# A hand-ordered two-layer kernel: list figures and ranks, weight preparation by pairs of blocks, sums in place, and a residual that stays on chip

## The chip, the cores and the metric

The kernel runs on one core of a Trainium2 chip. The metric is the device time of one execution in microseconds. Three executions of the kernel before took 1379.39, 1375.03 and 1376.81 us, a median of 1376.81. One further execution was profiled; its own time was 1382.9 us.

A core has five engines that run side by side, each through its own instructions in order: TensorE (PE in the profile; its weight loads are PEld), VectorE (DVE), ScalarE (ACT), GpSimd (POOL) and SyncE (SP), which in this kernel issues nearly all transfers between the chip's memory (SBUF) and device memory. Matmul results go into the eight banks of PSUM.

## The reference

The same two blocks, with the same weights, are applied twice to an activation of 2048 tokens by 640 columns, all in float32:

```python
    x = A_x
    x = x + _A_ref(_layernorm(x, axis=-1), A_wqkv, A_wo)
    x = x + _B_ref(_layernorm(x, axis=-1), B_w1, B_b1, B_w2, B_b2)
    x = x + _A_ref(_layernorm(x, axis=-1), A_wqkv, A_wo)
    x = x + _B_ref(_layernorm(x, axis=-1), B_w1, B_b1, B_w2, B_b2)
```

`_A_ref` is linear attention with 32 heads of 20 columns: q, k, v = x @ wqkv; phi(t) is t + 1 where t > 0 and exp(t) elsewhere, plus 1e-6; for each head the output is phi(q) @ (phi(k)^T v), divided by phi(q) times the sum of phi(k) over the tokens; then @ wo. `_B_ref` is a feed-forward block of 1728 columns: h = relu(x @ w1 + b1) squared, then h @ w2 + b2.

## The kernel before, in words

**Precision.** A float32 matrix is split into a high part in a shorter format (ScalarE copies it) and the rest as a low part (VectorE subtracts), and a product is three matmuls: high by low, low by high, high by high. `split` (L284) does this; on the way a split is always one ScalarE instruction and then one VectorE instruction.

**Tiles.** The 2048 tokens are 16 tiles of 128 rows. Four tiles make a group, so there are four groups.

**Attention, first half: the token loop (L901 to L1090).** For each tile t: layer norm, transpose, k and q by matmuls (`part`, whose products are issued in `mm3`, L574), phi of both, and the sums over tokens: G = x^T k (`g_part`), GT (`gt_part`, every second tile), and acc, the sum of phi(k) (`k_post`, L857). phi(q) is stored to device memory. In some tiles (`LATE`) the q part is left for later (`late_q`). The order of the instructions on each engine is that of the program text. The loop's tile 15 also splits wo (`wo_high`, `wo_low`), whose pieces `load_vo` (L748) loads in tiles 13 to 15. After the loop acc is split (`ah`) and multiplied by ones, on the way to the denominators; G becomes the per-head products and then one 640 by 640 matrix M per layer.

**Weight preparation, layer 0 only.** Beside the token loop `Prep` (L412) loads w1 and w2 in pieces, combines and splits them and stores the split units to device memory, from where both layers later reload them. Two neighbouring column blocks of w1 make a pair with four units: wE and wF are split as loaded; then four GpSimd operations (`sums`, L443) combine the two blocks, and wH and wG are split from that. The remaining w1 and w2 pieces are one unit each: 36 units in all, in an order `todo`. `PREP` says how many units each tile takes. In tile t a unit's load for tile t + 1 is issued (`load`), ScalarE and VectorE split this tile's units (`high`, `low`), and at the start of the next tile `store` puts the issue of their stores on SP's queue, where each waits for VectorE's low part. After that store the tile's other transfers are issued: kept q/k weights (`keep_kq`), from tile 13 on phi(q) (`b_load_pq`, four pieces of a tile each) and the pieces of wv and wo (`load_vo`).

**Between the halves.** For the first group, attention's output is multiplied by M and added to the input (`b_x1`), normalized, transposed (tiles 0 and 1 by block moves, 2 and 3 by TensorE in `f_trans`, L1352) and split (`f_split`). The feed-forward block uses one level of Strassen's scheme, so sums of transposed tiles are formed for pairs of tiles (`t_sums`, L1336, four VectorE operations into two fresh buffers tu and tv of the ring "f") and split (`t_split`). The ring "f" has twelve buffers of one tile (`F_BUFS`); an instruction that needs a thirteenth waits until one is free.

**Feed-forward and the rest of attention: an order planned as a list (L1896 to L2287).** For each group, 14 column blocks of h: blocks 12 and 13 directly (`fc1`, L1461), the others in six Strassen blocks of two, each in five segments with copies and adds between them (`Strassen`, L1482). Each block of h is then multiplied by its part of w2 (`fc2_tile`, L1638) into five accumulators of the group. While a group is in work, the attention output of the next groups' tiles is made (`q_line`, `pair_line` with products in one PSUM bank, `x_line`). The order on every engine is worked out when the program is built, by `Clock` (L81): each strand of work is a `Line`, a generator that yields its next step with the engine and a length; `Clock.next` takes for each engine the step with the smallest (start rounded to 0.1 us, rank), and `Clock.run` does the same for TensorE by (wait, rank). The steps are then issued in that order. The lengths are figures in the code: `cost`, `pe_cost`, and for transfers `go` (L150):

```python
                start = max(start, self.lanes.pop(0))
                self.t["DMA"] = max(self.t["DMA"], start + 1.3) + each / 0.39
                line.got = self.got = self.t["DMA"] + 0.7 + HOP
                self.lanes.append(line.got)
                start += 0.08
```

`lanes` are eight: an issue waits for the transfer that was issued eight before it. On the chip SP's queue is in order: an issue that waits holds up everything behind it.

**Weights in the feed-forward block.** `uses` (L370) is the order in which units are reloaded; `Units` (L483) reloads the next one (L503) as soon as TensorE has done with a buffer. There are three buffers, then a fourth, and a fifth ("b") after the attention pools are closed.

**The residual.** For the second half, x after attention is needed once more, with b2 added. `x_line` stores it for the later groups (`x1_keep`, L847); for the first group `f_bias` (L839) adds b2 in place in the tile's "f" buffer, stores it to `x1d`, and `x1_load` (L1749) reloads the group's four tiles into `x1s[g]` (L1752). `x1_line` does the reload for every group, and fc2's last block (L2222) waits for it. b2 is also held as a column, `b2col` (L268), one value per partition, loaded by `late_consts` and used by `preset`.

## Time and profile before

| | |
|---|---|
| median of three runs | 1376.81 us |
| the profiled execution, its own time | 1382.9 us |
| its span in the trace | 1381.2 us |
| VectorE, ScalarE, GpSimd busy | 982.9, 770.5, 147.2 us |
| moved by DMA | 316.11 MB, 229 GB/s over the span |
| mean granted TensorE clock | 0.994 |

How to read the profile: a line of the timeline or of a group names the kernel's line, the engine, the operation, what it writes and reads (out<-in, without buffer numbers) and the shapes; "x6" means six instructions merged. In square brackets stands how long the engine was idle before, and what ended that (the releaser, found from the semaphores). A timeline line begins with its start and its length in us. SPq is SP's sequencer; a DMA line there is the issue of a transfer, not the transfer. The token loop of layer 0 lies up to about 200 us, its feed-forward block from about 260 to 700, the token loop of layer 1 from there to about 880, its feed-forward block from about 940 to the end.

### The profile page before, as it was taken

Reading aid. Unit: us, or ns where it says so; the run is one execution under the profiler, and the core shown is the slowest. Engines: PE = TensorE matmul, PEld = TensorE weight load, DVE = VectorE, ACT = ScalarE, POOL = GpSimd, SP = SyncE. Lnnn points to the kernel's source line nnn. Section 1 sums busy time; section 2 is a strip of 40 time slices with the busy share of each in tenths; the row PEclk is TensorE's granted clock in tenths of the full one; section 3 lists DMA queues with packets and bytes.
Section 4 is the critical chain, followed back from the end, with each engine's and each line's share of the span. In section 5 each row is a group of like instructions: output and inputs, shape, how many; then the busy total and the mean of one; then the engine's idle time right before and its main releaser. Section 6 shows DMA issues by size and latency. Waiting matters only on the chain.

```text
span 1381.2 us, 21322 instructions
## 1 busy us (share of the span) xinstructions
PE 1337.4 (97%) x7616; PEld 1180.7 (85%) x7616; DVE 982.9 (71%) x1928; ACT 770.5 (56%) x1753; POOL 147.2 (11%) x196
## 2 busy tenths in 40 slices
PE   9999989989999999999999999999899999999999
PEld 8888879878888879888888889997788888898887
DVE  8888968887887787354256678799788876874323
ACT  5888845646664655446336687565365644554421
POOL 2334310000000000000012232100000000000000
PEclk9999999999999999999999999999999999999999
DMA  6679685397779768698731114166877788587684
GB/s 200 226 267 333 245 274 181 123 350 240 250 248 307 282 201 307 239 375 306 266 127 44 58 39 132 52 193 229 304 242 221 253 303 265 184 298 273 229 313 175
DMA packets 120240, 316.11 MB, mean 229 GB/s; under 512 B 15110, under 2 KB 40326, under 8 KB 119462
## 3 DMA queue, kind: packets, MB, share of 16 engines
q1 hardware_dynamic: 118622, 312.06, 65.4%
q10 hardware_dynamic: 1512, 2.69, 0.7%
q8 instruction: 60, 0.98, 0.3%
q14 instruction: 46, 0.38, 0.1%
HBM read 251.28 MB, written 64.85 MB: 229 GB/s over the span
## 4 chain that ended last, share of the span: by engine, by line
PE 71%; DMA 12%; DVE 11%; issue 2%; SPq 2%; ACT 1%; POOL 1%; ACTq 0%; DVEq 0%; POOLq 0%
PE PS L574 25%; PE PS L1659 21%; PE PS L1510 15%; PE PS L1520 4%; DMA pqt<-pq 4%; DMA u<-kept_wH 2%; PE PS L1476 2%; DMA u<-kept_w 2%; DMA u<-kept_wG 1%; SPq L773 1%; DMA u<-kept_wE 1%; PE PS L1188 1%; DVE bn L524 1%; DVE uprep L407 1%; PE PS L927 1%
## 5 line engine op out<-in xcount | busy, mean ns | idle before, releaser
L1659 PE MATMUL PS<-u,h 128*128 128x512 f32 x1318 | 346.1, 397 | 1.4 <-ACT s L1532 0.7
L562 ACT ACTIVATE z<-y 32x160 f32<-32x160 f32 x767 | 256.1, 334 | 88.4 <-DVE y L549 69.3
L574 PE MATMUL PS<-kq,xT 128*128 128x320 f32 (+2 forms) x1575 | 283.4, 334 | 4.3 <-DVE r L686 3.5
L1659 PEld LDWEIGHTS PS<-u,h 128*128 128x128 f32 x1318 | 241.1, 190 | 50.3 <-DMA u<-kept_w 1.0
L574 PEld LDWEIGHTS PS<-kq,xT 128*128 128x128 f32 x1575 | 250.0, 188 | 31.5 <-DVE r L686 3.8
L1510 PE MATMUL PS<-tx,u 128*128 128x256 f32 x1152 | 162.7, 284 | 11.1 <-DMA u<-kept_wH 5.9
L1510 PEld LDWEIGHTS PS<-tx,u 128*128 128x128 f32 x1152 | 151.4, 192 | 16.9 <-DMA u<-kept_wH 6.5
L1588 ACT ACTIVATE hr<-PS,b1sb 128x512 f32<-128x512 f32 x104 | 71.2, 685 | 140.9 <-PE PS L1520 123.2
L1510 PEld LDWEIGHTS PS<-xTb,u 128*128 128x128 f32 x864 | 120.5, 189 | 20.1 <-DVE PS L1552 6.8
L1510 PE MATMUL PS<-xTb,u 128*128 128x256 f32 x864 | 127.4, 283 | 7.2 <-DVE PS L1552 4.6
L574 PE MATMUL PS<-kh,xh 128*128 128x512 f32 x480 | 126.9, 398 | 0.0
L529 POOL TENSOR_SCALAR rs<-mv 128x1 f32<-128x1 f32 x62 | 30.5, 492 | 831.0 <-DVE mv L526 831.0
L574 PEld LDWEIGHTS PS<-kh,xh 128*128 128x128 f32 x480 | 88.1, 190 | 15.7
L1594 DVE TENSOR_TENSOR hr<-hr 128x512 f32<-128x512 f32 x71 | 48.7, 687 | 73.6 <-ACT h L1607 73.3
L677 ACT ACTIVATE e<-PS 128x320 f32<-128x320 f32 (+4 forms) x128 | 53.2, 434 | 83.5 <-PE PS L574 71.1
L1607 ACT ACTIVATE h<-hr 128x512 fp32r<-128x512 f32 x104 | 65.0, 629 | 62.3 <-PE PS L1659 61.0
L1659 PE MATMUL PS<-h,u 128*128 128x512 f32 x328 | 94.0, 395 | 0.0
L1597 DVE TENSOR_TENSOR h<-hr,h 128x512 fp32r<-128x512 f32 x104 | 70.9, 685 | 11.4 <-ACT hr L1592 7.4
L685 DVE TENSOR_SCALAR e<-e 128x320 f32<-128x320 f32 (+4 forms) x128 | 41.5, 325 | 50.8 <-ACT e L677 50.3
L1520 PE MATMUL PS<-xTb,u 128*128 128x512 f32 x288 | 76.1, 394 | 0.0
L1659 PEld LDWEIGHTS PS<-h,u 128*128 128x128 f32 x328 | 59.9, 188 | 12.3
L864 POOL TENSOR_TENSOR acc<-acc,r 128x640 f32<-128x640 f32 x28 | 50.7, 1810 | 176.8 <-DVE r L686 176.8
(178 smaller groups left out, 1889.6 us busy)
## 6 DMA issues: line engine op xcount, KB each, us to landing
u<-kept_w SPq DMA_DIRECT2D x116, 640.0 KB, 5.5
u<-kept_wE SPq DMA_DIRECT2D x48, 512.0 KB, 4.3
u<-kept_wH SPq DMA_DIRECT2D x48, 512.0 KB, 5.1
u<-kept_wG SPq DMA_DIRECT2D x48, 512.0 KB, 5.3
u<-kept_wF SPq DMA_DIRECT2D x48, 512.0 KB, 5.2
x<-x SPq DMA_DIRECT2D x48, 320.0 KB, 5.6
pqt<-pq SPq DMA_DIRECT2D x128, 80.0 KB, 5.3
x<-xr SPq DMA_DIRECT2D x32, 320.0 KB, 3.6
```

Of the source, the lines that this page charges most:

```text
L562: nc.scalar.activation(d, v, AF.Copy)
L574: nc.tensor.matmul(ps, a, b, start=first and i == 0, stop=last and i == 2)
L677: nc.scalar.activation(self.e[:, a:b], ps, AF.Exp)
L685: nc.vector.tensor_scalar(e, e, 1.0, PHI_EPS, op0=ALU.min, op1=ALU.add)
L864: nc.gpsimd.tensor_tensor(out=acc, in0=acc, in1=r, op=ALU.add)
L1510: nc.tensor.matmul(ps, l[:, d], r[:, d], start=start and d == 0 and n == 0, stop=d == 1 and n == 2, skip_group_check=True,)
L1520: nc.tensor.matmul(ps, l[:, k], r, start=False, stop=n == 2, skip_group_check=True)
L1588: nc.scalar.activation(r, ps, AF.Relu, bias=b1sb[:, c : c + 1])
L1594: nc.vector.tensor_tensor(out=r, in0=r, in1=r, op=ALU.mult)
L1597: nc.vector.tensor_tensor(out=h[:, 1], in0=r, in1=h[:, 0].bitcast(F32), op=ALU.subtract)
L1607: yield "ACT", cost("ACT", GT), lambda: nc.scalar.activation(h[:, 0], r, AF.Square)
L1659: nc.tensor.matmul(ps, l, r, start=(first or new) and k == 0, stop=end and k == len(a) - 1, **loose)
```

## The change

- `PREP_ORDER` writes the units' order by hand: "a1" is wE and wF of pair 1, "b1" its wH and wG, "r" the next of the remaining pieces. An "a" part's two units now stand next to each other, and so do a "b" part's; pieces of w2 and w1 stand between. `PREP` gives 3, 4, 4, 3, 4, 4, 4, 4, 4, 1, 0, 1 units to tiles 2 to 13; before it was 3 to each of tiles 2 to 12, and 4 in tiles 3, 5 and 7.
- `k_post`: acc's sum of tile 15 (both layers) and of tile 9 (layer 0) goes to VectorE instead of GpSimd.
- `t_sums` works in the two buffers that it reads; tu and tv are gone. In `f_trans` the copy of the transposed tile stands between the two halves of the split, on ScalarE for both tiles, and for tile 3 two of the first sums follow it. `T_FIRST` writes out the order of the first sums and splits.
- The first group's residual: `f_bias` adds b2 from the "f" buffer straight into `x1s[0]`; the four stores and the four reloads of that group are gone. `b2col` becomes a third column of the tile `scalars`.
- In `uses` unit 12 of w2 of the first group comes ahead of wE and wH.
- `Clock`: an issue counts 0.42 instead of 0.08 us, a transfer starts after 1.2 instead of 1.3, moves 0.35 instead of 0.39 MB per us, and lands 1.0 instead of 0.7 later. Every line's rank comes from a table per layer, `RANK`, with a second number `early` that is taken off the start (or the wait) before lines are compared; the starting times of some lines come from the table as well (`at`).

The diff, cut:

```diff
-PREP = {t: 4 if t in (3, 5, 7) else 3 for t in range(2, 13)}
+PREP_ORDER = "a0 r b0 a1 b1 r r a2 r b2 a3 b3 r r a4 r r b4 a5 b5 r r r r"
+PREP = dict(zip(range(2, 14), (3, 4, 4, 3, 4, 4, 4, 4, 4, 1, 0, 1)))
...
+RANK = (
+    dict(
+        full=(0, 0.0), half=(4, 0.0), moves=(4, 0.0), unit=(8, 0.0), next=(9, -0.5), preset=(9, 0.2),
+        strip=(6, 0.0), bias=(8, 0.0), fc1=(2, 0.0), fc2=(4, 0.8), q0=(6, 0.0), q1=(8, 0.0), pair=(1, 0.0),
+        load_x=(6, 0.0), x0=(5, 0.0), x1=(4, 0.0), t=(3, 0.0), x1_load=(0, 0.0), late=(7, 0.8),
+        mixed=(4, 0.0), ring=(1, 0.0), kq=(2, 0.0), at=(4.5, 4.8, 2.0, 13.0),
+    ),
+    dict(
+        full=(0, 0.0), half=(2, 0.0), moves=(4, 0.0), unit=(8, -0.2), next=(5, 0.0), preset=(3, 0.0),
+        strip=(8, 0.0), bias=(3, -0.5), fc1=(3, 0.0), fc2=(4, 0.0), q0=(7, 0.2), q1=(8, 0.0), pair=(1, 0.0),
+        load_x=(6, 1.5), x0=(3, 0.2), x1=(6, 0.0), t=(1, 0.4), x1_load=(2, 0.2), late=(3, 0.0),
+        mixed=(6, 0.0), ring=(1, -0.2), kq=(2, 0.0), at=(4.8, 3.5, 2.0, 10.5),
+    ),
+)
+T_FIRST = "0 u0 2 0 v0 2 u0 2 u2 v0 2 v2 u2 v2"
...
-        return 0.08 if h[0] == "SP" else h[1]
+        return 0.42 if h[0] == "SP" else h[1]
...
-                self.t["DMA"] = max(self.t["DMA"], start + 1.3) + each / 0.39
-                line.got = self.got = self.t["DMA"] + 0.7 + HOP
+                self.t["DMA"] = max(self.t["DMA"], start + 1.2) + each / 0.35
+                line.got = self.got = self.t["DMA"] + 1.0 + HOP
                 self.lanes.append(line.got)
-                start += 0.08
+                start += 0.42
...
-            key = (round(at, 1), line.rank)
+            key = (round(at - line.early, 1), line.rank)
...
-                    key = (max(line.pe - now, 0.0), line.rank)
+                    key = (max(line.pe - now - line.early, 0.0), line.rank)
...
-    scalars = cpool.tile([P, 2], F32, name="scalars")
-    neghalf, one = scalars[:, 0:1], scalars[:, 1:2]
+    scalars = cpool.tile([P, 3], F32, name="scalars")
+    neghalf, one, b2col = (scalars[:, i:i + 1] for i in range(3))
...
-                    u[2], u[3] = u[3], u[2]
+                    u.insert(0, u.pop(2))
...
         def f_bias(t):
-            v = xr.pop(t)
-            nc.vector.tensor_tensor(out=v, in0=v, in1=b2bc, op=ALU.add)
-            yield
-            nc.sync.dma_start(x1d[t], v)
+            nc.vector.tensor_tensor(out=x1s[0][:, t], in0=xr.pop(t), in1=b2bc, op=ALU.add)
...
-            elif not (layer == 0 and t in (1, 2)):
-                nc.gpsimd.tensor_tensor(out=acc, in0=acc, in1=r, op=ALU.add)
+            elif not (layer == 0 and t in (1, 2, 9)):
+                eng = nc.vector if t == NT - 1 else nc.gpsimd
+                eng.tensor_tensor(out=acc, in0=acc, in1=r, op=ALU.add)
...
-            u, v = ftile("tu"), ftile("tv")
+            tsum[t] = zr, zl
             for out, x, y in (
-                (v[:, a], zr[:, a], zl[:, a]),
-                (u[:, a], zr[:, b], zr[:, a]),
-                (u[:, b], zr[:, b], v[:, a]),
-                (v[:, b], zl[:, b], u[:, b]),
+                (zl[:, a], zr[:, a], zl[:, a]),
+                (zr[:, a], zr[:, b], zr[:, a]),
+                (zr[:, b], zr[:, b], zl[:, a]),
+                (zl[:, b], zl[:, b], zr[:, b]),
             ):
...
-            f_split(t, ps)
-            xz[t] = ftile("xz")
-            if t == 2:
-                nc.vector.tensor_copy(xz[t][:, : 4 * P], ps[:, : 4 * P])
-            else:
+            def keep():
+                xz[t] = ftile("xz")
                 nc.scalar.activation(xz[t][:, : 4 * P], ps[:, : 4 * P], AF.Copy)
+                if also:
+                    also()
+
+            f_split(t, ps, keep)
...
         def x1_line():
-            for g in range(NG):
-                if g > 0:
-                    yield "need", ("strip", g - 1)
+            for g in range(1, NG):
+                yield "need", ("strip", g - 1)
                 yield "need", *(("b", TG * g + i) for i in range(TG))
...
-        main = ck.add(fc1_line(), 2)
-        fc2 = ck.add(fc2_line(), 3)
+        main = ck.add(fc1_line(), R["fc1"])
+        fc2 = ck.add(fc2_line(), R["fc2"])
...
-        ck.add(x1_line(), 9)
-        ck.add(late_line(), 1, 7.5)
+        ck.add(x1_line(), R["x1_load"])
+        ck.add(late_line(), R["late"], R["at"][2])
```

96 lines of the change are left out of this document (47 added, 49 removed).

## The prediction

> **What bounds the kernel now.** I read the page first: its head, and the busy time of the engines.
>
> ```profile
> span 1381.2 us, 21322 instructions
> PE 1337.4 (97%) x7616; PEld 1180.7 (85%) x7616; DVE 982.9 (71%) x1928; ACT 770.5 (56%) x1753; POOL 147.2 (11%) x196
> ```
>
> TensorE is busy for 1337.4 of 1381.2 us. No edit removes a matmul, so all that can be won is the idle 43.8 us, and what a slow clock costs. Next, the busy time by stretches of the span (start:end, length, then PE, PEld, DVE, ACT, POOL with their instructions, granted clock, DMA share, GB/s): the end of the token loop of layer 0, the first feed-forward group of layer 0 and the rest of them, the token loop of layer 1, and again the first group and the rest.
>
> ```profile
> 150.00:205.00 55.00, 46.74 (x258) 41.77 (x257) 44.72 (x83) 32.62 (x72) 16.80 (x15) 0.97 0.76 254
> 260.50:345.00 84.50, 76.21 (x427) 66.50 (x426) 69.69 (x130) 41.90 (x90) 2.21 (x4) 0.96 0.79 276
> 345.00:700.00 355.00, 348.55 (x1981) 305.03 (x1980) 222.99 (x446) 184.67 (x413) 13.86 (x29) 1.00 0.78 274
> 700.00:939.50 239.50, 239.50 (x1377) 215.72 (x1376) 182.02 (x361) 154.76 (x377) 49.82 (x52) 1.00 0.29 90
> 939.50:1025.00 85.50, 77.24 (x440) 66.80 (x440) 70.86 (x132) 42.95 (x92) 2.20 (x4) 0.98 0.79 273
> 1025.00:1381.20 356.20, 345.31 (x1972) 301.94 (x1970) 214.58 (x432) 161.27 (x352) 9.06 (x20) 1.00 0.73 252
> ```
>
> Idle PE by stage: 8.26, 8.29, 6.45, 0, 8.26 and 10.89 us. Layer 1's token loop, which prepares no weights, has none: what layer 0 loses there belongs to the preparation. The granted clock falls below 1.00 in the stages with the longest waits. Then the timeline of each engine around the waits, below.
>
> **A. Weights by pairs, preparation ahead (layer 0, tiles 2 to 13).** TensorE's three waits at the end of the loop (last bracket: idle before, and its releaser):
>
> ```profile
> 162.05 1.15 PE L574 MATMUL PS<-xh,kh 128*128 128x320 f32 x6 [2.27 <-DVE r L686]
> 196.47 2.46 PE L574 MATMUL PS<-kq,xT 128*128 128x320 f32 x15 [3.53 <-DVE r L686]
> 200.81 0.85 PE L1133 MATMUL PS<-ah,ones 128*128 128x320 f32 x4 [1.88 <-DVE ah L287]
> ```
>
> The first, in tile 12: VectorE was in eight block copies while GpSimd summed the last weight pair; the same eight copies alone, in tile 14, are the second line.
>
> ```profile
> 155.50 4.24 DVE L560 COPY z<-y 32x160 f32<-32x160 f32 x8
> 175.41 2.11 DVE L560 COPY z<-y 32x160 f32<-32x160 f32 x8
> 156.17 3.18 POOL L457 TENSOR_TENSOR st<-st 128x256 f32<-128x256 f32 x4
> ```
>
> In the new order the last "a" part is units 29 and 30 of 36, and the counts 3, 4, 4, 3, 4, 4, 4, 4 of tiles 2 to 9 add up to 30: its sums run in tile 9, and tile 12 prepares nothing. That returns 4.24 - 2.11 = 2.1 of the 2.27 us. The other two come out of SP's queue (a wait of SP, then ScalarE):
>
> ```profile
> SPq L410 <- DVE uprep L407: 14.7, 5, 13.7
> 187.47 0.74 ACT L891 ACTIVATE uo<-uraw 120x640 fp32r<-120x640 f32 x1 [1.91 <-DMA uraw<-wod]
> 192.78 0.74 ACT L891 ACTIVATE uo<-uraw 120x640 fp32r<-120x640 f32 x1 [3.19 <-DMA uraw<-wod]
> ```
>
> The store of tile 12's units holds SP for 13.7 us, and the q loads, v and wo stand behind it; ScalarE then waits 1.91 + 3.19 us for wo, the exponential that frees TensorE's bank behind that. With nothing prepared in tile 12 that store is gone, and tile 13's loads go up to 13.7 us sooner. One unit is left in tile 13; its store, in tile 14, waits for VectorE and again has q and wo loads behind it, but one store instead of three ahead of them. The last acc sum moves from GpSimd to VectorE, ahead of kh's low half there; that half is needed only after the 15 matmuls of 196.47, so the sum is covered, and the chain to ah gets no longer. So 2.1 + 3.53 + 1.88 = 7.5 us can go, and some clock time, for which these rows:
>
> ```profile
> 201.50 3.80 PE L574 MATMUL PS<-kh,xh 128*128 128x512 f32 x9
> 305.21 2.56 PE L1659 MATMUL PS<-u,h 128*128 128x512 f32 x6
> 333.16 1.56 PE L1659 MATMUL PS<-u,h 128*128 128x512 f32 x6
> ```
>
> Six 512-column matmuls take 1.56 us, but 2.56 behind a wait; nine take 3.80, where 9/6 of 1.56 is 2.34. So the waits cost 1.5 us more here and 1.0 at 305. A is at most 9.0; if wo lands only little sooner, 3. I take 7; late next are wo's last loads again, which ScalarE may still meet for a microsecond.
>
> The Trainium skill (TensorE: Matmul & The Clock Gate, Part 1: The HAM clock gate) has the clock halved only after an idle window of about 3.4 us. By that the 1.0 us behind the wait of 1.87 us (row below) would not be won with it, and C would be 2 smaller; the measured 2.56 us speaks against the rule here.
>
> **B. Sums in place, and the copy between the split's halves.** Both feed-forward stages begin with a wait for ScalarE's split of the last tile, and ScalarE had waited for a buffer that VectorE's sums held:
>
> ```profile
> 261.83 5.95 PE L1476 MATMUL PS<-xTb,u 128*128 128x512 f32 x25 [0.83 <-ACT xTb L286]
> 940.90 5.95 PE L1476 MATMUL PS<-xTb,u 128*128 128x512 f32 x25 [0.83 <-ACT xTb L286]
> 260.05 0.44 ACT L677 ACTIVATE e<-PS 128x320 f32<-128x320 f32 x1 [2.60 <-DVE tu L1348]
> ```
>
> Without tu and tv the "f" ring gives two buffers fewer, so those 2.60 us shrink; the copy that moves from VectorE to ScalarE fits into them. Bounds 0 and 1.66 for both layers; I take 1.5; late next is TensorE itself, with the last q part ahead of fc1.
>
> **C. First residual kept on chip.** It removes four stores and four loads of 320 KB per layer from SP. The waits for weights in the first groups, SP's issues before them, and the stores (x8 for both layers: min/median/max ns):
>
> ```profile
> 288.62 0.95 PE L1510 MATMUL PS<-tx,u 128*128 128x256 f32 x6 [1.16 <-DMA u<-kept_wG]
> 302.97 0.98 PE L1510 MATMUL PS<-tx,u 128*128 128x256 f32 x6 [1.87 <-DMA u<-kept_wH]
> 967.89 0.94 PE L1510 MATMUL PS<-tx,u 128*128 128x256 f32 x6 [0.79 <-DMA u<-kept_wG]
> 982.12 0.97 PE L1510 MATMUL PS<-tx,u 128*128 128x256 f32 x6 [2.25 <-DMA u<-kept_wH]
> 284.38 7.60 SPq L773 DMA_DIRECT2D pqt<-pq  x8
> 292.99 2.15 SPq L1752 DMA_DIRECT2D x<-x  x4
> L844 SPq DMA_DIRECT2D x<-xr x8: 319/320/960, 276.0 to 960.7; - x8
> ```
>
> The wH of 302.97 was issued right after the four reloads (2.15 us), and those behind eight q loads that took 7.60 us, because an issue waits for the transfer eight before it and four of these were the stores. 2.6 MB less at the stage's 276 GB/s is 9.5 us of DMA time; each wait is under 2.3. The four waits are 6.07 us; with the 1.0 of clock after 302.97, and as much allowed in layer 1 (granted 0.98), 8.1. Late next are the hand-offs inside a Strassen block, three waits of TensorE for its own copies and adds:
>
> ```profile
> 269.96 0.97 PE L1510 MATMUL PS<-tx,u 128*128 128x256 f32 x6 [0.75 <-ACT s L1532]
> 271.45 0.98 PE L1510 MATMUL PS<-xTb,u 128*128 128x256 f32 x6 [0.52 <-ACT PS L1538]
> 274.39 0.97 PE L1510 MATMUL PS<-xTb,u 128*128 128x256 f32 x6 [0.53 <-DVE PS L1552]
> ```
>
> They are there today beside the weight waits, and q loads may move up into the freed slots. Bounds 2 and 8.1; I take 5. The bias column's move, and w2's unit 12 ahead of wE, I cost at nothing: the same bytes, one slot earlier.
>
> **D. The list: SP's issue at 0.42 instead of 0.08 us, ranks per layer.** Rows above give 0.32 to 0.54 us per issue (2.15 for four), so the new figure is true. What a plan that is too early costs: VectorE, in order, stands before a q load that has not landed, and TensorE waits behind it.
>
> ```profile
> DVE pr L784 <- DMA pqt<-pq: 20.7, 13, 3.7
> 1172.23 1.14 PE L574 MATMUL PS<-uT,uS 128*128 128x320 f32 x6 [2.43 <-DVE uu L1839]
> ```
>
> By the code, the last of the four parts of a q load (109 KB planned each) was due 1.3 + 4 x 0.28 + 0.77 = 3.2 us after the first issue, and is now due 3 x 0.42 + 1.2 + 0.31 + 1.07 = 3.8 us after: 0.6 later, where the mean lateness is 20.7 / 13 = 1.6. So about a third of what hangs on this goes. The later groups' idle is 6.45 + 10.89 = 17.3 us; perhaps half of it hangs on loads: 3 us. The ranks reorder the rest with a sign that no row shows. Bounds: 12 won, 8 lost.
>
> **E. What preparing earlier adds.** Tiles 8, 9 and 10 take four units instead of three, and tile 9 an acc sum on VectorE. Tiles 7 and 8 were here, a unit is a load and a store:
>
> ```profile
> 106.00:118.00 12.00, 12.00 (x63) 10.24 (x62) 10.78 (x20) 10.41 (x27) 6.16 (x7) 1.00 0.99 361
> st<-in_B_w_dram SPq DMA_DIRECT2D x26, 320.0 KB, 4.6
> kept_w<-uprep SPq DMA_DIRECT2D x11, 640.0 KB, 6.0
> ```
>
> The DMA is full (0.99, 361 GB/s), VectorE has 1.2 us free and TensorE never waits. A unit more is up to 960 KB, 2.7 us at 361 GB/s; three are 8. Cover is the one tile that loads run ahead. Bounds 0 and 8; I take 1, for TensorE was busy for 12.00 of 12.00 us.
>
> **Sum.** -7 - 1.5 - 5 - 3 + 1 = -15.5 us against the profiled execution (span 1381.2, its time 1382.9). That execution is 6 us above the median of 1376.81; I take the difference over to the median: 1361.3 us.
>
> **Rivals.**
> *Slower: uncovered hand-offs.* Where no fc2 work fills it, a block waits three times, the 0.75, 0.52 and 0.53 us of the rows in C: 1.8 us, and there are 48 blocks. Told that weights land later, the list may spend fc2 work ahead of a block instead of inside it. From nine such blocks the gain is gone (15.5 / 1.8); at twelve it is +6, 1383. For it: nothing but the first blocks shows it today. Against: fc2 keeps its place behind fc1 in the ranks. 0.14.
> *The freed slots are filled again* by q and x loads, and the ranks bring nothing: C and D 0, so -7 - 1.5 + 1 = -7.5, 1369. For it: eight q loads stood waiting for slots. 0.20.
> *The DMA is full in tiles 8 to 10:* E at +8, -8.5 in all, 1368. For it the 0.99, against it the unbroken TensorE. 0.12. The Trainium skill (DMA: Bandwidth & Descriptors, Specifications) gives about 358 GB/s as a core's share of HBM, so by it nothing is left in that stage; the row with 361 agrees.
> *The bias column ties up its tile.* If its load counts as a write of the whole tile, the first power waits for it:
>
> ```profile
> 5.20 0.55 POOL L530 TENSOR_TENSOR rs<-rs,scalars 128x1 f32<-128x1 f32 x1 [2.92 <-DVE rs L529]
> 10.50 0.33 SPq L275 DMA_DIRECT2D b2col<-in_B_b_dram  x1
> ```
>
> at least 10.8 - 5.2 = 5.6 us plus the landing, some 11 in all: -4.5, 1372. Against it: PS is one tile of eight banks, and TensorE writes it while others read it. 0.02.
>
> **How the numbers follow.** The forecast has 0.52. Its own range: half-widths A 3, C 3, D 10, E 3, together about 11 (root of the squares): 1350 to 1372. With the rivals, 1348 to 1375 leaves out the slower one and a tail. About 0.3% (4 us; the three runs spread over 4.4) can be told from no change. Faster by more: forecast and the two rivals at -7.5 and -8.5, less their edges, 0.81; within 0.07; slower 0.12.
>
> **What would show it.** A: no waits over 0.5 us at tiles 12 and 15, clock 1.00 at 200. B: fc1 starts without its 0.83. C: no x store or reload in the first groups, waits for wG and wH under 0.5. D: the wait of L784's counterpart for q loads falls from 20.7 to under 15. Wrong if hand-off waits appear in many blocks, if TensorE idles between 100 and 150, or if the first groups keep their 8 us.

## The result, and the profile after

The changed kernel takes 1333.28 us (median of four runs, 1331.96 to 1334.40), the kernel before 1378.10 on the same chip: a ratio of 0.9665 with a 95% interval of 0.9641 to 0.9689. The forecast was 1361.3 us and its range 1348 to 1375. The sign was right and the gain came out three times as large, 44.8 us instead of 15.5. The profiled execution took 1331.96 us with a span of 1330.3 us.

The head of the page and the engines, then the chain that ended last:

```profile
span 1330.3 us, 21345 instructions
PE 1315.6 (99%) x7616; PEld 1176.4 (88%) x7616; DVE 979.8 (74%) x1934; ACT 770.8 (58%) x1750; POOL 141.7 (11%) x193
...
PE 87%; DMA 5%; DVE 4%; ACT 2%; issue 1%; SPq 1%; POOL 0%; DVEq 0%; ACTq 0%; POOLq 0%
```

TensorE's idle time fell from 43.8 to 14.7 us, which is 29.1 of the 50.9 us between the two spans. The other 21.8 us are *busy* time: the same 7616 matmuls take 1315.6 us instead of 1337.4. The second part was almost wholly missing from the prediction.

The same by stages, feed-forward of layer 0 (first group, rest), token loop of layer 1, feed-forward of layer 1 (first group, rest); columns as in the prediction:

```profile
250.80:335.00 84.20, 82.41 (x497) 74.38 (x496) 73.89 (x145) 42.86 (x89) 3.30 (x6) 1.00 0.79 265
335.00:668.40 333.40, 331.63 (x1907) 294.07 (x1906) 219.97 (x437) 179.76 (x406) 12.02 (x27) 1.00 0.82 286
668.40:849.20 180.80, 180.80 (x972) 159.54 (x970) 130.61 (x257) 119.52 (x298) 43.62 (x43) 1.00 0.25 74
907.50:992.00 84.50, 81.41 (x485) 72.41 (x484) 72.37 (x141) 43.12 (x88) 1.96 (x4) 1.00 0.79 271
992.00:1330.30 338.30, 333.25 (x1925) 295.74 (x1923) 211.63 (x421) 161.71 (x354) 11.06 (x20) 1.00 0.75 258
```

The granted clock is 1.00 in every stage. The first groups idle 1.8 and 3.1 us (before 8.29 and 8.26), the later ones 1.8 and 5.1 (before 6.45 and 10.89). Layer 1's token loop had no idle time before and has none now, and yet it is about 1 us shorter: what changed there cannot be a wait.

The waits: what is left of TensorE's for weights and of VectorE's for q loads (total, times, longest), and the two longest single waits of TensorE behind the token loop of layer 0:

```profile
PE PS L1679 <- DMA u<-kept_w: 0.6, 1, 0.6
PE PS L1530 <- DMA u<-kept_wG: 0.4, 1, 0.4
DVE pr L805 <- DMA pqt<-pq: 6.1, 5, 2.3
...
1015.35 5.98 PE L1496 MATMUL PS<-xTb,u 128*128 128x512 f32 x25 [1.03 <-DVE xTb L1822]
1094.40 0.98 PE L1530 MATMUL PS<-xTb,u 128*128 128x256 f32 x6 [1.01 <-DVE PS L1572]
```

The same waits of TensorE in the kernel before:

```profile
PE PS L1510 <- DMA u<-kept_wH: 5.9, 3, 2.3
PE PS L574 <- DVE uu L1839: 5.1, 5, 2.4
PE PS L574 <- DVE xr L1839: 4.5, 6, 1.5
PE PS L1510 <- DMA u<-kept_wG: 3.7, 4, 1.2
PE PS L1659 <- DMA u<-kept_w: 0.7, 2, 0.4
```

TensorE waited 10.3 us for weights and 9.6 us for the parts uu and xr that VectorE makes behind the q loads. Now it is 1.0 and 1.8 us.

### The profile page after: what moved, and what is told of

Its sections match the earlier page's. It is cut to its first block, busy times and chain, and to the rows that moved or that the text cites. A ratio compares the mean times of both kernels' runs of the same rounds, so it can differ in the third digit from the quotient of the medians.

```text
span 1330.3 us, 21345 instructions
## 1 busy us (share of the span) xinstructions
PE 1315.6 (99%) x7616; PEld 1176.4 (88%) x7616; DVE 979.8 (74%) x1934; ACT 770.8 (58%) x1750; POOL 141.7 (11%) x193
## 4 chain that ended last, share of the span: by engine, by line
PE 87%; DMA 5%; DVE 4%; ACT 2%; issue 1%; SPq 1%; POOL 0%; DVEq 0%; ACTq 0%; POOLq 0%
PE PS L595 32%; PE PS L1679 25%; PE PS L1530 16%; PE PS L1540 4%; PE PS L1496 3%; PE PS L616 3%; DMA pqt<-pq 2%; ACT z L583 1%; PE PS L1207 1%; DMA u<-kept_w 1%; PE PS L1236 1%; PE PS L946 1%; DVE uprep L425 1%; DMA u<-kept_wG 1%; SPq L794 0%
## 5 line engine op out<-in xcount | busy, mean ns | idle before, releaser
L1679 PE MATMUL PS<-u,h 128*128 128x512 f32 x1318 | 338.7, 390 | 1.3 <-ACT PS L1686 0.8
L1530 PE MATMUL PS<-tx,u 128*128 128x256 f32 x1152 | 161.7, 283 | 2.0 <-ACT s L1552 1.5
L1530 PEld LDWEIGHTS PS<-tx,u 128*128 128x128 f32 x1152 | 150.7, 191 | 6.3 <-ACT s L1552 1.9
L1530 PEld LDWEIGHTS PS<-xTb,u 128*128 128x128 f32 x864 | 120.7, 190 | 12.2 <-ACT PS L1558 2.2
L1530 PE MATMUL PS<-xTb,u 128*128 128x256 f32 x864 | 126.7, 283 | 2.6 <-ACT PS L1558 1.6
L595 PEld LDWEIGHTS PS<-kh,xh 128*128 128x128 f32 x480 | 87.0, 188 | 14.7 <-DVE kh L886 0.2
L1562 DVE TENSOR_TENSOR PS<-PS,s 128x256 f32<-128x256 f32 x48 | 20.7, 431 | 63.7 <-ACT PS L1558 63.6
```

Of the source, the lines that this page charges most:

```text
L595: nc.tensor.matmul(ps, a, b, start=first and i == 0, stop=last and i == 2)
L1530: nc.tensor.matmul(ps, l[:, d], r[:, d], start=start and d == 0 and n == 0, stop=d == 1 and n == 2, skip_group_check=True,)
L1679: nc.tensor.matmul(ps, l, r, start=(first or new) and k == 0, stop=end and k == len(a) - 1, **loose)
```

## The experiments

All runs in one table. Stage lengths are differences of the start times of each stage's first matmul in the trace; "loop" is the token loop and "FF" the feed-forward stage of a layer. The last three columns are TensorE's waits, all of a kind added up from the rounded rows of the waits view: for weights (released by a DMA), for the input of a group's fc1 (released by VectorE's xTb), and for uu and xr. All are in us; the kernel before took 1379.6 to 1380.8 beside these runs. The time is the median of a kernel's runs, all other columns come from the one profiled execution, which in e2 (1355.8 us) and e10 (1336.6 us) was 6 and 5 us below the median.

| run | time | loop 0 | FF 0 | loop 1 | FF 1 | weights | fc1 input | uu, xr |
|---|---|---|---|---|---|---|---|---|
| before | 1380 | 199.4 | 437.8 | 181.9 | 440.3 | 10.3 | 0.0 | 9.6 |
| after | 1333.3 | 191.0 | 417.6 | 180.8 | 422.7 | 1.0 | 1.0 | 1.8 |
| e1_column_own | 1335.5 | 191.6 | 420.3 | 181.9 | 421.8 | 1.6 | 0.9 | 0.6 |
| e2_old_figures | 1362.1 | 191.0 | 431.8 | 180.8 | 432.3 | 12.3 | 2.6 | 2.6 |
| e3_old_ranks | 1350.5 | 191.9 | 431.3 | 180.8 | 426.3 | 1.2 | 5.8 | 4.9 |
| e4_old_list | 1355.3 | 191.2 | 433.1 | 180.8 | 429.1 | 8.9 | 0.0 | 5.2 |
| e5_round_trip | 1356.2 | 191.3 | 435.5 | 180.8 | 430.8 | 3.4 | 11.4 | 4.8 |
| e6_old_prep | 1340.8 | 197.0 | 420.1 | 180.8 | 424.0 | 2.6 | 0.8 | 4.7 |
| e7_residual_alone | 1371.4 | 199.1 | 437.3 | 181.9 | 432.1 | 8.7 | 1.2 | 10.3 |
| e8_prep_alone | 1371.1 | 191.7 | 434.5 | 181.9 | 440.4 | 8.1 | 0.0 | 9.6 |
| e9_list_alone | 1366.6 | 198.8 | 434.4 | 181.9 | 427.3 | 1.9 | 11.4 | 1.5 |
| e10_issue_038 | 1341.6 | 191.0 | 417.8 | 180.8 | 427.1 | 1.1 | 0.0 | 6.2 |
| e11_issue_046 | 1340.1 | 191.2 | 421.2 | 180.8 | 425.9 | 2.6 | 2.6 | 1.5 |
| e12_pad_64 (one run) | 1338.9 | 191.6 | 421.5 | 181.5 | 424.4 | 1.3 | 1.5 | 4.2 |
| e13_sum_buffers | 1334.2 | 191.3 | 419.3 | 180.8 | 422.3 | 0.4 | 1.5 | 2.7 |
| e14_acc_gpsimd | 1334.6 | 191.5 | 418.5 | 180.8 | 424.4 | 1.0 | 2.4 | 1.8 |
| e15_pad_96 (one run) | 1341.9 | 192.5 | 421.6 | 181.9 | 426.1 | 1.9 | 2.1 | 3.5 |
| e16_pad_128 (one run) | 1338.1 | 191.8 | 420.9 | 181.4 | 424.0 | 1.2 | 1.1 | 3.4 |
| e17_landing_2 | 1354.9 | 191.4 | 421.0 | 180.8 | 442.8 | 1.3 | 10.6 | 3.1 |
| e18_old_ranks_landing_2 | 1336.3 | 191.1 | 423.1 | 180.8 | 422.2 | 4.2 | 0.0 | 0.5 |

### The list: figures and ranks undone, one by one and together

e2 takes the old figures into the changed kernel, e3 the old ranks and start times, e4 both.

```diff
-        return 0.42 if h[0] == "SP" else h[1]
+        return 0.08 if h[0] == "SP" else h[1]
...
-                self.t["DMA"] = max(self.t["DMA"], start + 1.2) + each / 0.35
-                line.got = self.got = self.t["DMA"] + 1.0 + HOP
+                self.t["DMA"] = max(self.t["DMA"], start + 1.3) + each / 0.39
+                line.got = self.got = self.t["DMA"] + 0.7 + HOP
...
-                start += 0.42
+                start += 0.08
```

```diff
-RANK = (
...
+RANK = 2 * (
     dict(
+        full=(0, 0.0), half=(0, 0.0), moves=(4, 0.0), unit=(2, 0.0), next=(9, 0.0), preset=(2, 0.0),
+        strip=(8, 0.0), bias=(6, 0.0), fc1=(2, 0.0), fc2=(3, 0.0), q0=(6, 0.0), q1=(7, 0.0), pair=(1, 0.0),
+        load_x=(6, 0.0), x0=(5, 0.0), x1=(4, 0.0), t=(3, 0.0), x1_load=(9, 0.0), late=(1, 0.0),
+        mixed=(8, 0.0), ring=(1, 0.0), kq=(2, 0.0), at=(4.5, 4.8, 7.5, 12.0),
     ),
 )
```

> The changed kernel, its list planned with the figures of before (0.08 us an issue, 1.3, 0.39 MB per us, 0.7), ranks and all else as changed. Theory 'figures': the waits in the feed-forward blocks (27 us of idle TensorE in the profile before, about 8 after) went because loads are planned when they land; then this kernel loses most of it, 15 us or more, and VectorE waits for q loads about 20 us again. Rival 'ranks': the order among lines did it; then it loses under 5 us. Rival 'lanes': the residual that stays on chip did it; under 5 us as well.

> The changed kernel with the ranks and starting times of before for both layers and no early allowance, figures and all else as changed. Theory 'figures': under 5 us lost. Rival 'ranks': 15 us or more lost, with waits at the places where they were before. Rival 'lanes': under 5 us.

> The changed kernel with both the figures and the ranks of before; the residual on chip, the sums in place, the order of w2's unit 12 and the preparation as changed. If figures and ranks act each for itself, its loss is the sum of the two runs above. 'Lanes' expects under 5 us (about 1338), 'figures' and 'ranks' expect 15 to 25 us (about 1350 to 1358) with the first groups' waits for weights still gone.

Measured: e2 1362.09 us (0.9869 of the kernel before, 0.9833 to 0.9905), e3 1350.51 (0.9788, 0.9763 to 0.9813), e4 1355.34 (0.983, 0.9788 to 0.9872). The list as a whole is therefore worth 22 of the 47 us (1380 less 1333.3; beside the changed kernel itself the kernel before took 1378.1, so the whole is 45 to 47). Its two halves don't add up: with the old ranks the new figures win 5 us, with the new ranks 29; the new ranks lose 7 us under the old figures and win 17 under the new ones. The 5 and the 7 are not clear of the noise, since the intervals of e4 and e3 overlap, and so do those of e4 and e2; the 29 and the 17 are. Where the time goes is in the waits of TensorE. e4 first, with both old, then e2:

```profile
PE PS L1524 <- DMA u<-kept_wH: 4.6, 4, 3.0
PE PS L1524 <- DMA u<-kept_wG: 3.3, 4, 1.1
PE PS L1673 <- DMA u<-kept_w: 1.0, 2, 0.6
```

```profile
PE PS L1530 <- DMA u<-kept_wG: 9.6, 6, 3.2
PE PS L1530 <- DMA u<-kept_wH: 2.4, 2, 2.2
```

With the old figures TensorE waits 8.9 and 12.3 us for weights, with the new ones (e3, after) 1.2 and 1.0, whatever the ranks. The whole table splits in this way: 8.1 us or more in the five kernels with the old figures, 4.2 or less in the fifteen with new ones. Which of the four figures does it was not taken apart. The residual is kept on chip in all four kernels, so the slots and bytes of its transfers do not make these waits. They stand in e4's first groups too (2.1 and 1.4 us), where its expectation had them gone. What e3 has instead is a wait for the next group's input:

```profile
369.85 3.95 PE L1490 MATMUL PS<-xTb,u 128*128 128x512 f32 x10 [4.07 <-DVE xTb L1816]
```

### The list alone, on the kernel before

e9 puts the new figures and ranks into the kernel before (the edits above, the other way round, with the ranks passed to every line) and changes nothing else.

> The kernel before with the list alone: the new figures for transfers and the new ranks, and nothing else of the change (preparation, sums, residual and column as before). Additive theory: the list is worth the 22 us that the changed kernel loses with the old list, 1358 where the kernel before takes 1380. Rival (the ranks were fitted to the changed kernel's own list of work, as the run with the round trip suggests, which lost 23 us where the two removed transfers alone gained 9): under 10 us, 1370 or more, or even slower than before, with long waits of TensorE in the feed-forward stages.

Measured: 1366.55 us, 0.9904 (0.9877 to 0.9931), 14 us less than before. It lies between the two theories. The weight waits are gone here too (1.9 us), though the residual makes its round trip and the preparation is the old one. But at the first change of group TensorE stands still for longer than in any other place of these runs:

```profile
381.69 7.64 PE L1491 MATMUL PS<-xTb,u 128*128 128x512 f32 x25 [9.71 <-DVE xTb L1817]
```

Layer 1, which has no such wait of this size, takes 427.3 us instead of 440.3, layer 0 434.4 instead of 437.8.

### The residual: its round trip again, and kept alone

e5 gives the changed kernel its stores and loads back; e7 takes them out of the kernel before.

```diff
-            nc.vector.tensor_tensor(out=x1s[0][:, t], in0=xr.pop(t), in1=b2bc, op=ALU.add)
+            v = xr.pop(t)
+            nc.vector.tensor_tensor(out=v, in0=v, in1=b2bc, op=ALU.add)
+            yield
+            nc.sync.dma_start(x1d[t], v)
...
-            for g in range(1, NG):
-                yield "need", ("strip", g - 1)
+            for g in range(NG):
+                if g > 0:
+                    yield "need", ("strip", g - 1)
```

> The changed kernel with one part undone: the first residual goes through HBM again, four stores and four loads of 320 KB per layer. Prediction's theory (C: slots and bytes of the DMA queue): the first groups lose 2 to 8 us, about 5, and the waits for wG and wH of 0.8 to 2.3 us are back there; 1338 us. Rival (the weights were late in the first groups because the list did not know when they land; with true figures it plans round the eight transfers): under 2 us, 1334 to 1335, and no wait for a weight over 0.5 us. Second rival (the ranks were fitted to a list without these transfers, and any other list under them loses more than the transfers cost): over 8 us, 1342 or more, with waits in later groups too, where no such transfer runs.

> The kernel before with one part alone: the first residual stays on chip. Prediction's theory (C): the waits for wG and wH in the first groups go, 2 to 8 us, about 5: 1375 on a chip where the kernel before takes 1380. Rival (the old list puts q loads into the freed slots and the weights stay late): within 2 us of the kernel before, the waits in the first groups still there. If it is more than 8 us, a list that does not know its landings was held up by these transfers in the later groups too.

Measured: e5 1356.15 us (0.9822, 0.9787 to 0.9857), 22.9 more than the changed kernel; e7 1371.42 (0.9932, 0.9908 to 0.9956), 8.9 less than before. Alone, the residual wins a little more than the prediction's upper bound of 8.1 us. The first groups of e7:

```profile
261.50:344.00 82.50, 78.17 (x468) 69.67 (x469) 72.06 (x135) 42.84 (x91) 2.41 (x5) 1.00 0.76 261
940.00:1024.00 84.00, 80.40 (x476) 71.10 (x477) 73.44 (x138) 42.88 (x91) 3.30 (x6) 1.00 0.77 263
```

They idle 4.3 and 3.6 us instead of 8.3 each. Of their waits for weights about half is left, 2.0 and 1.0 us against 3.1 and 3.3: those for wH are gone, single ones for wG of 1.6 and 0.7 us are there. In layer 1 the whole stage keeps this gain (432.1 us against 440.3), in layer 0 it is lost again behind the first group (437.3 against 437.8), where the list came out in another order.

In e5 the transfers themselves cannot cost 22.9 us. The timelines of TensorE, the changed kernel first and then e5, show the largest piece of what does:

```profile
350.27 2.88 PE L1679 MATMUL PS<-u,h 128*128 128x512 f32 x12
352.99 2.43 PE L1496 MATMUL PS<-xTb,u 128*128 128x512 f32 x10
355.25 0.84 PE L1679 MATMUL PS<-h,u 128*128 128x512 f32 x3
355.94 3.56 PE L1496 MATMUL PS<-xTb,u 128*128 128x512 f32 x15
359.33 2.88 PE L1679 MATMUL PS<-u,h 128*128 128x512 f32 x12
```

```profile
353.57 2.88 PE L1682 MATMUL PS<-u,h 128*128 128x512 f32 x12
356.29 1.52 PE L1682 MATMUL PS<-h,u 128*128 128x512 f32 x6
357.65 2.88 PE L1682 MATMUL PS<-u,h 128*128 128x512 f32 x12
370.24 7.57 PE L1499 MATMUL PS<-xTb,u 128*128 128x512 f32 x25 [9.71 <-DVE xTb L1825]
379.07 2.11 PE L1682 MATMUL PS<-u,h 128*128 128x512 f32 x8 [1.26 <-DVE h L1624]
```

In the changed kernel fc1 of the second group (xTb,u) begins at 353 with fc2 work of the first group (u,h and h,u) still left to put between. In e5 that work is spent at 360.5, and VectorE and ScalarE are still at the transposes of the second group's input: 9.71 us of nothing. The wait is the same in e9, which has the new list (figures and ranks) and the round trip in common with e5. So it belongs to the new list on a kernel with the round trip, and not to the eight transfers as such: with them under the old list, in the kernel before, no fc1 waits for VectorE. Whether the figures or the ranks make it, no run separates.

### The preparation: undone, and alone

e6 takes the old order and counts into the changed kernel, e8 the new ones into the kernel before.

```diff
-PREP_ORDER = "a0 r b0 a1 b1 r r a2 r b2 a3 b3 r r a4 r r b4 a5 b5 r r r r"
-PREP = dict(zip(range(2, 14), (3, 4, 4, 3, 4, 4, 4, 4, 4, 1, 0, 1)))
+PREP = {t: 4 if t in (3, 5, 7) else 3 for t in range(2, 13)}
```

> The changed kernel with the old order and counts of weight preparation in layer 0's token loop. Prediction's theory (A and E: the late preparation makes the waits at tiles 12 and 15): layer 0's token loop gets 6 to 9 us longer, all of the 8.4 us by which it got shorter, with waits of about 2 us at tile 12 and of 3.5 and 1.9 us at the end of the loop; 1340 us. Rival (the sum for which VectorE took over from GpSimd, and the copies, made the gain, and the order only moves work that is covered): under 2 us, 1334 to 1335. The stages behind the loop stay as they are by both.

> The kernel before with one part alone: weights prepared by pairs in the new order and counts. Prediction's theory (A and E): 6 to 8 us less, all in layer 0's token loop, whose waits of 2.27, 3.53 and 1.88 us go: 1373 where the kernel before takes 1380. Rival (the acc sums and the copies are needed for it too: GpSimd still sums in tile 14 and 15 and ScalarE still waits for wo): 3 us or less, and one or two of the three waits remain.

Measured: e6 1340.80 us (0.9717, 0.9682 to 0.9751), 7.5 more than the changed kernel; e8 1371.11 (0.9941, 0.9912 to 0.9969), 9.2 less than before. The token loop of layer 0 gets 6.0 us longer in e6 and 7.7 shorter in e8, and in e6 the three waits are back in their places:

```profile
161.67 1.96 PE L591 MATMUL PS<-xh,kh 128*128 128x320 f32 x6 [2.41 <-DVE r L703]
...
194.69 2.46 PE L591 MATMUL PS<-kq,xT 128*128 128x320 f32 x15 [1.48 <-DVE r L703]
198.38 0.85 PE L1148 MATMUL PS<-ah,ones 128*128 128x320 f32 x4 [1.23 <-DVE ah L304]
```

SP and ScalarE show the cause: SP's longest wait for a unit's low part (uprep) is 13.7 us before, 3.3 in the changed kernel and 13.6 in e6, and ScalarE's waits for wo are 6.3, 0.5 and 4.2 us. e6 issues TensorE's matmuls in the changed kernel's order, and e8 in that of the kernel before, so nothing of either comes from another list. The trace of e8 is 3.3 us shorter than that of the kernel before in layer 0's feed-forward stage as well; its order being the same, that is the clock (three stretches at half clock there before, one in e8; see the part on the clock).

### Sums and running sum

e13 gives the sums their own buffers tu and tv again and puts the copy back behind the split, e14 puts the running sum of tiles 9 and 15 back on GpSimd.

```diff
-            tsum[t] = zr, zl
+            u, v = ftile("tu"), ftile("tv")
...
-            f_split(t, ps, keep)
+            f_split(t, ps)
+            xz[t] = ftile("xz")
...
+                yield "f", 2
```

```diff
-            elif not (layer == 0 and t in (1, 2, 9)):
-                eng = nc.vector if t == NT - 1 else nc.gpsimd
-                eng.tensor_tensor(out=acc, in0=acc, in1=r, op=ALU.add)
+            elif not (layer == 0 and t in (1, 2)):
+                nc.gpsimd.tensor_tensor(out=acc, in0=acc, in1=r, op=ALU.add)
```

> The changed kernel with the sums in two buffers of their own again (and the copy of a tile behind both halves of its split). Prediction's theory (B): the wait of 0.83 us of fc1's start is back in both layers and the stretch between the token loop and fc1 gets 1 us longer, 58.4 to 59.4 us in each layer; 0 to 1.7 us in all by this. Rival (ranks fitted to one list): the list in the feed-forward stages has to find two buffers more and comes out in another order, and these stages lose 7 to 20 us besides, as with the issue figure moved by a tenth (7 to 8 us) or with the round trip (23).

> The changed kernel with the running sum of tiles 9 and 15 on GpSimd again. Prediction's reckoning (the sum is covered either way): within 2 us, and no wait of TensorE over 0.5 us at tiles 9, 12 and 15. Rival (GpSimd's sum at tile 15 ends late and ah waits for it): the wait ahead of the last products of 1.9 us is back at the end of layer 0's token loop, 2 to 4 us with the clock, and the same in layer 1. The feed-forward stages stay as they are, since their list is the same.

Measured: e13 1334.21 us (0.9663, 0.9636 to 0.9689) and e14 1334.57 (0.9666, 0.9634 to 0.9697), 0.9 and 1.3 us more than the changed kernel, about as much as the runs spread. In e13 both starts of fc1 wait again:

```profile
252.14 5.96 PE L1493 MATMUL PS<-xTb,u 128*128 128x512 f32 x25 [0.84 <-ACT xTb L302]
...
911.91 5.95 PE L1493 MATMUL PS<-xTb,u 128*128 128x512 f32 x25 [1.15 <-ACT xTb L302]
```

The stretches between token loop and fc1 are 59.4 and 59.7 us, against 58.4 and 58.3 in the changed kernel. The rival did not come: the two buffers were never what the list lacked, and TensorE's order is the same. e14 shows no wait over 0.5 us at tiles 9, 12 and 15; the sum was covered, as reckoned.

### The column's place, and where buffers lie

e1 gives the bias column its tile of 32 bytes per partition again; e12, e15 and e16 keep it in the changed place and add an unused tile of 64, 96 and 128 bytes behind the bias tile. Every buffer allocated later moves by as much.

```diff
-    scalars = cpool.tile([P, 3], F32, name="scalars")
-    neghalf, one, b2col = (scalars[:, i:i + 1] for i in range(3))
+    scalars = cpool.tile([P, 2], F32, name="scalars")
+    neghalf, one = scalars[:, 0:1], scalars[:, 1:2]
...
+    b2col = cpool.tile([P, 1], F32, name="b2col")
```

```diff
     b1sb = cpool.tile([P, NF], F32, name="b1sb")
+    pad = cpool.tile([P, 16], F32, name="pad")
+    nc.vector.memset(pad, 0.0)
```

> The changed kernel with b2's column in a tile of its own again, so that everything allocated after it lies where it lay before; nothing else differs. In the two profiles the 512-column matmuls stand 231.4 ns apart before and 228.9 after where they follow each other directly, 2.5 ns x 3172 = 8 us. Theory 'addresses': the pace belongs to where the operands lie, so this kernel has 231 ns and is about 8 us slower than the changed one (1341). Rival 'execution': the pace is that of the chip or the execution, this kernel is like the changed one within 2 us (1333), and the kernel before, on the same chip, has whatever pace this one has.

> The changed kernel with an unused tile of 64 bytes per partition behind the bias tile, so that all buffers allocated after it lie 64 bytes higher; one look for the pace of TensorE. In the kernel before and with the column in a tile of its own, which lies 32 bytes higher, 512-column matmuls back to back took 231.3 ns, in the changed kernel 228.9, and layer 1's token loop, without waits in any of them, 181.9 and 180.8 us. Theory (the address by 64 bytes decides): 228.9 ns and 180.8 us again. Rival (any shift, or 128 bytes, decides): 231 ns and about 181.9 us, or a third value.

> The unused tile with 96 bytes, one look for the pace. Shifts so far: 0 gave 228.9 ns for a 512-column matmul and 180.8 us for layer 1's token loop, 32 gave 231.3 and 181.9, 64 about 230 and 181.5. If the pace goes by the address within 128 bytes this is the fourth value, within 228 to 232; below 228.5 ns and 180.5 us it would be a faster place than the changed kernel's.

> The unused tile with 128 bytes. Theory (the address within 128 bytes decides): 228.9 ns and 180.8 us again, as without it, and the stages as in the changed kernel. Rival (a longer period, or which buffers lie far apart): another value, 230 or more.

Measured: e1 1335.54 us (0.9684, 0.9661 to 0.9707), 2.3 more than the changed kernel, with intervals that overlap; one run each of e12, e15 and e16 took 1338.91, 1341.93 and 1338.14. All four issue TensorE's matmuls in the changed kernel's order. Layer 1's token loop, in which TensorE never waits, by stretches of e1, e12, e15 and e16:

```profile
671.80:853.60 181.80, 181.80 (x971) 159.39 (x969) 130.60 (x257) 119.52 (x298) 43.64 (x43) 1.00 0.24 74
```

```profile
672.90:854.40 181.50, 181.50 (x973) 159.38 (x971) 130.74 (x257) 119.59 (x298) 43.74 (x43) 1.00 0.24 74
```

```profile
673.90:855.80 181.90, 181.90 (x972) 159.41 (x970) 130.73 (x257) 119.69 (x298) 43.90 (x43) 1.00 0.25 74
```

```profile
672.70:854.00 181.30, 181.30 (x971) 159.60 (x969) 130.69 (x257) 119.55 (x298) 43.78 (x43) 1.00 0.24 74
```

The clock is 1.00 in all of them; the changed kernel's loop takes 180.80. Two 512-column matmuls in a row start 228.9 ns apart in the changed kernel (mean over some 2900 such pairs of the trace), 231.3 in e1 and 231.4 before, 230.3, 231.6 and 230.6 with 64, 96 and 128 bytes. The chip does not make it: e2 to e6 on the chip of e1, and e13 and e14 on that of e15 and e16, have the changed kernel's addresses and 228.9 to 229.2. So the pace goes with the address, as the theory 'addresses' had it, though not its 8 us: 256-column matmuls are 0.6 ns faster in e1 (118.7 against 119.3), and its waits are fewer. A period of 64 or 128 bytes, which two of the expectations had as their theory, is refuted. What it is in the address remains open.

### One figure moved, and a landing nearer to the measured one

e10 and e11 set the issue on SP to 0.38 and 0.46 us instead of 0.42. e17 adds 1 us to the landing, in the changed kernel, and e18 does the same with the old ranks (on e3).

```diff
-                line.got = self.got = self.t["DMA"] + 1.0 + HOP
+                line.got = self.got = self.t["DMA"] + 2.0 + HOP
```

> The changed kernel with one figure of the list moved by a tenth: 0.38 instead of 0.42 us for an issue on SP; ranks and all else unchanged. Theory that true figures make the gain: 0.38 is as near to the measured 0.32 to 0.54 us as 0.42, so within 3 us of the changed kernel, 1331 to 1336. Rival (the ranks are fitted to this one list, and any list under them that comes out differently in order is an ordinary draw): 8 to 20 us more, 1341 to 1353, with new waits of TensorE over 1 us in the later groups.

> As the run before with the figure moved the other way, 0.46 us. True figures: within 3 us of the changed kernel, 1331 to 1336. Fitted ranks: 8 to 20 us more, 1341 to 1353. If only one of the two runs is slow, the order that comes out decides and not the distance from the true figure.

> The changed kernel with one more figure moved: a load counts as there 2.0 instead of 1.0 us after its bytes (last part of a q load 4.8 us after the first issue, where the profile shows 4.9 for a part); ranks unchanged. Theory that truth makes the gain: at or below the changed kernel, 1328 to 1334, with less than its 6.1 us of VectorE's waits for q loads. Rival (the ranks are fitted to one order): 1340 to 1356, like the other lists that come out in another order, even though fewer waits for q loads remain.

> The same figure with the old ranks. Truth by itself: as the step from old to new figures gave 5 us with these ranks (1355.3 to 1350.5), this one gives some more, 1343 to 1349. Rival (without ranks to go with it, the order is an ordinary draw): 1348 to 1358, above or below 1350.5 with no sign to be told beforehand.

Measured: e10 1341.60 us (0.9718, 0.9682 to 0.9754), e11 1340.13 (0.9714, 0.9682 to 0.9747), e17 1354.94 (0.9807, 0.9774 to 0.984), e18 1336.25 (0.9672, 0.9632 to 0.9712). A tenth more or less on one figure costs 7 to 8 us (e10's and e11's intervals begin at 0.9682, the changed kernel's ends at 0.9689), and the truer landing costs 21.7 us with the new ranks: these act as if fitted to one order. VectorE's waits for q loads come to 8.5 us in e17, where the theory of truth had less than 6.1. The loss of e17 is in layer 1, in two starts of fc1:

```profile
1030.05 8.19 PE L1496 MATMUL PS<-xTb,u 128*128 128x512 f32 x25 [4.83 <-DVE xTb L1822]
...
1147.49 7.54 PE L1496 MATMUL PS<-xTb,u 128*128 128x512 f32 x25 [5.77 <-DVE xTb L1822]
```

The median landing of a q load's part in the changed kernel (KB each, us from issue to landing):

```profile
pqt<-pq SPq DMA_DIRECT2D x128, 80.0 KB, 4.9
```

With the old ranks, in contrast to the new ones, each step of the figures towards the measured landing helped: 1355.3, 1350.5, 1336.3 (only the second step is clear of the noise). e18 comes within 3 us of the changed kernel without any new rank, and none of its fc1 starts waits for VectorE. Both theories of the expectations are half right: the new ranks behave as fitted ones, and they are not needed for most of the gain. Whether e18's order owes more to the figure than to chance, one kernel cannot tell; its result is better than its theory's range.

## Why the prediction was right or wrong

**A and E, preparation: right.** Taken as -7 + 1 = -6, measured -9.2 alone and +7.5 undone. The mechanism is shown, with the same three waits coming and going with the order. The rest is in the stretch behind the loop, 1.7 us shorter in e8, where the clock had been low. What the earlier units add is E's 1 us: two new waits for VectorE of 0.49 and 0.51 us, at 138 and 143 us of the changed kernel. By the prediction's own words idle time between 100 and 150 was a sign of being wrong; it came, at the size that E had.

**B, sums in place: right in its mechanism.** Taken as 1.5, bounds 0 and 1.66; the two stretches gain 1.0 and 1.3 us, 0.6 more than the upper bound, and the timed difference of 0.9 is not clear of the noise.

**C, residual: right in size alone, but its waits were not its own.** Taken as 5 with bounds 2 and 8.1; alone it gives 8.9. The waits for weights in the whole kernel, though, are still 8.7 us in e7 and 8.9 in e4, where the residual is on chip, and 1.9 in e9, where it is not. Of the four waits of 6.07 us that C counted in the first groups, the two for wH (4.1 us) went with the residual and the two for wG stayed (1.6 and 0.7 us in e7). The late weights hung on the list's figures more than on the slots, and the prediction put them down to C alone.

**D, the list: the step that failed.** It was to give 3 us, with 12 won and 8 lost as bounds, worked out as a third of half of 17.3 us. The lateness of q loads went as said (20.7 us of VectorE's waits to 6.1, under the 15 that was named), but the term took q loads as all that a list's figure can reach. It reaches every weight as well: 10.3 us of waits for weights and 9.6 for uu and xr stood in the trace of before, and 14.1 us came from the list alone, 22 beside the rest. The sign of the ranks "that no row shows" depends on the figures as far as the medians go: -17 us with the new ones, +7 with the old, of which only the first is clear of the noise. How the 22 us divide among the four figures and the ranks stays open. The signs that were to show D, C, B and A right all came; none of them tested D's size.

**The ceiling was wrong.** "All that can be won is the idle 43.8 us, and what a slow clock costs" leaves out that TensorE's busy time itself can fall without a slow clock. The 21.8 us that it fell have three parts. The granted clock rose from 0.994 to 1.000, which is 8.3 us of 1381.2: the trace of before has five stretches of 3.4 us at half clock, from 201.6, 290.3, 304.0, 638.5 and 983.2 us. The prediction had seen three of them and allowed 1.5, 1.0 and 1.0 us, because it read only the first six or nine matmuls; the one at 638.5 hides in a stage whose clock is rounded to 1.00:

```profile
638.50:641.90 3.40, 2.98 (x8) 2.42 (x9) 0.00 (x0) 1.09 (x4) 0.00 (x0) 0.50 1.02 421
```

Then the pace of the matmuls: e1, with the same order and clock, has 1321.9 us of PE busy against 1315.6, so 6.3 us, of which its idle time gives back 2.8. The remaining 7 us are the edges of the waits. The last matmul ahead of a wait counts as busy to its own (modelled) end and not to the next start, and the first two behind it start further apart than in a steady row; six 256-column matmuls right behind a wait take 0.98 us where 0.88 is usual. Summed over the traces this is 0.25 us for each wait, and the kernel before has 47 waits of TensorE, e1 18 (the changed kernel 20): 29 fewer, 7.1 us.

**The bias column's move, taken at nothing,** was wrong as well. No wait for its load shows, but the 32 bytes that it freed move every later buffer: 6.3 us of TensorE's busy time, 2.3 us of the timed difference (not clear of the noise), and the whole difference between 231.4 and 228.9 ns.

**The sum of the parts.** Alone: preparation 9.2, residual 8.9, list 14.1; undone: column 2.3, sums 0.9, running sum 1.3 (these three not clear of the noise). That is 36.7 of 47 us. Most of the other 10 is interplay: the list is worth 8 us more beside the rest than alone, where it makes the 9.71 us wait together with the residual's round trip. The place of w2's unit 12 was not tried by itself.

**The rivals.** Uncovered hand-offs in many blocks did not come: all waits of TensorE ahead of the Strassen products fell (L1510 before, L1530 after) from 18.2 to 4.5 us. Its mechanism in another place did: fc2 work spent too early leaves an uncovered start of fc1 (e3, e5, e9, e17), at up to 9.7 us a piece instead of 1.8, but not in the order that the changed kernel has. Freed slots that are filled again would have left C and D at nothing, which e7 and e4 refute. The full DMA queue did not cost E its 8 us, nor was 361 GB/s the most that it moves: the changed kernel has 367 GB/s between 106 and 118 us with TensorE busy for 12.00 of 12.00. And the bias column did not tie up its tile: its wait would have held the first tiles, and loop 0 is no longer in the changed kernel than in e1.

**The clock.** The same 25 matmuls behind a wait of the same length, in e2 and in e11:

```profile
1040.67 5.97 PE L1496 MATMUL PS<-xTb,u 128*128 128x512 f32 x25 [2.59 <-DVE xTb L1822]
```

```profile
1025.34 7.61 PE L1496 MATMUL PS<-xTb,u 128*128 128x512 f32 x25 [2.59 <-DVE xTb L1822]
```

A wait of 2.59 us costs nothing more in one and 1.64 us more in the other. The granted clock tells why. It changes only at whole steps of 3.41 us (numbers in the last section), so the time line has a grid of windows that a slow stretch of the same trace makes visible. In e11 one stretch is slow, the second of these two:

```profile
1023.30:1026.70 3.40, 1.36 (x6) 1.15 (x7) 3.30 (x8) 2.82 (x9) 0.00 (x0) 1.00 0.47 154
1026.70:1030.10 3.40, 3.40 (x10) 2.65 (x9) 1.45 (x5) 1.22 (x2) 0.00 (x0) 0.50 0.07 12
```

In e2 the slow stretch that begins at 960.5 us fixes the grid; 23 and 24 steps later, at 1039.0 and 1042.4, two windows end, and the wait lies across both:

```profile
1035.60:1039.00 3.40, 2.49 (x11) 1.72 (x10) 3.40 (x6) 2.61 (x5) 0.00 (x0) 1.00 0.46 154
1039.00:1042.40 3.40, 1.73 (x7) 1.43 (x8) 3.30 (x8) 2.49 (x7) 0.00 (x0) 1.00 0.52 154
```

TensorE is idle for 2.04 us of one window in e11, and for 0.91 and 1.67 us of two in e2: the same wait, cut differently by the grid. The Trainium skill (TensorE: Matmul & The Clock Gate, Part 1: The HAM clock gate) has a free-running window of 3.4 us and half the rate when it gates. By estimate from these two figures one window at half rate loses 1.7 us, and the 1.64 agrees. What the prediction took from it, that only a wait of about 3.4 us is punished, does not hold: some 1.9 us of idle time within one window were enough. So part of what is counted as clock here is luck: the grid does not lie the same in each execution. Of e4's four runs the fastest was granted 0.999 of the clock (1350.83 us) and the slowest 0.994 (1360.99).

## What to carry to other kernels

Where an order of work is planned ahead from figures, look up every wait that hangs on a planned time, weights too, before sizing a change of the figures; and try the figures with neutral ranks first, since ranks that fit one list were worth nothing here, or less, beside another. Undoing a part in a planned kernel also draws a new order, so compare the order and the waits before a difference is given to the part. Idle time of the bounding engine is no ceiling for a gain: price the slow matmuls behind the waits, the edges of the waits and the pace of its instructions beside it, and count the stretches at half clock in the trace itself, since a stage's mean clock hides a single one.

## What the runs showed of the hardware

The pace of fp32 matmuls of 512 columns depends on where the buffers lie: 228.9 to 231.6 ns per matmul over five shifts of 0 to 128 bytes per partition, at a granted clock of 1.00 and with no wait. Over the whole kernel TensorE's busy time ran from 1315.6 us (changed kernel) to 1324.2 (96 bytes), with the same instructions in the same order.

TensorE's clock halves for whole windows on a fixed grid. Thirteen of the traces have slow stretches within the kernel, 30 in all; each lasts one, two or three times 3.41 us, and within a trace they begin whole multiples of 3.41 us apart, to 0.01 us. What decides is TensorE's idle time in the window just ahead. Of the some 5000 windows of these grids behind the first 10 us, with the clock at 1.00, all 27 with 1.85 us of idle time or more were followed by a slow one, three of the 18 with 1.60 to 1.85 us were, and none of the rest. A slow window that is filled with matmuls loses half its length, 1.7 us. So the price of a wait is its length, 0.25 us at its edges, and either 1.7 us or nothing, by where it falls on the grid; a wait of under 1.6 us alone never had the 1.7 us behind it, but several within one window had (at 290.3 us of the kernel before, 1.68 us together).
